# Regrouping the last rows of the output projection's weights: loads of 2, 1 and 1 rows, and rows 26 and 27 as one load

One Trainium2 chip, one core. The metric is the device time of the whole kernel in microseconds (us); a kernel's figure is the median of its runs. PE is TensorE (PEld its weight loads), DVE is VectorE, ACT ScalarE, POOL GpSimd, SP SyncE; SPq and ACTq stand for DMAs issued from SP and ACT. A load has landed when its semaphore has got the arrival of the last of the sixteen DMA engines.

## The reference, cut

```python
B, Sq, D = 32, 4, 1024;  Hq, Hkv, Sk, Dh = 32, 4, 2048, 128      # all bf16
q = (x @ wq).reshape(B, Sq, Hq, Dh).transpose(0, 2, 1, 3)
k, v = repeat(k_cache, 8, axis=1), repeat(v_cache, 8, axis=1)
p = softmax(einsum("bhqd,bhkd->bhqk", q, k) * Dh ** -0.5)
o = einsum("bhqk,bhkd->bhqd", p, v)
return o.transpose(0, 2, 1, 3).reshape(B, Sq, Hq * Dh) @ wo      # wo: 4096 x 1024
```

151 MB must be read, nearly all of it the two caches. `wo`, 8 MB, comes last.

## The kernel before

Everything is loaded by one queue, issued from SP in a fixed order: x, wq, the K and V caches batch by batch, then `wo`. In SBUF `wo` is 32 "rows" of 1024 columns on each of 128 partitions; one row is one step of the contraction of the output projection.

```python
WO = (4, 4, 4, 4, 4, 4, 2, 1, 1)          # rows 0 to 27, whole rows, so many to a load
NA = 768                                  # rows 28 to 31 come as columns 0:768, then 768:1024
LATE = 4
NB = NA + 144
COLS = ((0, 0, NA // 2), (512, NA // 2, NA), (1024, NA, NB), (1536, NB, D))
# ... (cut)
pieces = [(sum(WO[:c]), m, 0, D) for c, m in enumerate(WO)] \
       + [(u, 1, 0, NA) for u in range(Hq - LATE, Hq)] \
       + [(Hq - LATE, LATE - 1, NA, D), (Hq - 1, 1, NA, D)]       # (first row, rows, columns)
for c, (u, m, n0, n1) in enumerate(pieces):
    # ... (cut)   one load for each piece, with a semaphore of its own
# ... (cut)   the products: PE waits for the piece that holds row u's columns
for u in range(Hq - LATE):
    oproj(u, (0, 1, 2, 3))
for js in ((0, 1), (2, 3)):               # all of 0:768 first, then 768:1024
    for u in range(Hq - LATE, Hq):
        oproj(u, js)
# ... (cut)   oproj_out: PSUM to SBUF, then two stores
for j, eng in enumerate(("dve", "act", "act", "dve")):
    copy(eng, *COLS[j], j)
for j, (n0, n1, waits) in enumerate(((0, NA, (0, 1)), (NA, D, (2, 3)))):
    p.dma(("sp", "act")[j], ... out_flat[:, n0:n1] <- y_sb[:, n0:n1] ..., [("oe", i) for i in waits], ...)
```

So the tail has two halves: the first store (768 columns, from SP) can go while the last 256 columns are still being loaded and multiplied; the second store (256 columns, from ACT) ends the kernel.

## Time and profile before

| | before |
|---|---|
| median of the first three runs | 362.21 us (362.02 to 362.26) |
| span of the profiled run (first to last instruction), granted clock | 360.8 us, 1.0 |
| bytes read, mean rate over the span | 151.26 MB, 420 GB/s |
| last `wo` piece landed (all sixteen engines' parts) | 358.20 us |
| first, second store issued | 358.65, 359.08 us |

The page and the tail's timeline stand in the prediction below.

### The profile page before, as it was taken

The numbers are of one execution on the slowest core, as the hardware profiler recorded it, in microseconds if no ns is written. First come the engines' busy times: TensorE is split into PE (matmuls) and PEld (weight loads), VectorE is DVE, ScalarE is ACT, GpSimd is POOL, SyncE is SP. The second block draws the span as 40 slices with busy tenths as digits, with TensorE's granted clock in tenths as the row PEclk, the third lists the DMA queues.
The fourth block names the chain that finished last, engine by engine and source line by source line (L and its number), as shares of the span: only waits on it lengthen the run. The fifth ranks groups of instructions, "written<-read, shape, count | busy, mean of one in ns | idle before, by whom it ended". The sixth has DMA issues, their size and how long they took to land. (4 is left out here: it accounts for less than half of the span.)

```text
span 360.8 us, 6288 instructions
## 1 busy us (share of the span) xinstructions
PE 307.0 (85%) x3066; PEld 147.2 (41%) x2342; DVE 269.2 (75%) x171; ACT 103.0 (29%) x111; POOL 165.3 (46%) x262
## 2 busy tenths in 40 slices
PE   1988788999999999988999888888888898889896
PEld 1002000445444554444444444443333444448721
DVE  0018799999899888879999888888888888865600
ACT  1014222333333333333333333323222233333100
POOL 8002055255555555554455444455555554444100
PEclk9999999999999999999999999999999999999999
DMA  8999999999999999999999999999999999999996
GB/s 323 434 434 430 425 427 430 430 419 425 431 425 427 429 429 429 426 429 430 429 425 430 430 425 429 429 432 421 432 427 434 420 432 429 434 420 430 414 417 242
DMA packets 12651, 151.66 MB, mean 420 GB/s; under 512 B 1376, under 2 KB 2656, under 8 KB 3168
## 3 DMA queue, kind: packets, MB, share of 16 engines
q1 hardware_dynamic: 12496, 151.46, 99.1%
q8 instruction: 6, 0.10, 0.1%
q10 hardware_dynamic: 144, 0.07, 0.1%
q14 instruction: 5, 0.04, 0.0%
HBM read 151.26 MB, written 0.26 MB: 420 GB/s over the span
## 5 line engine op out<-in xcount | busy, mean ns | idle before, releaser
L329 DVE STREAM_TRANSPOSE KT_sb<-big 128x2048 f32<-128x2048 f32 x64 | 146.6, 2293 | 16.5 <-DMA big<-in_k_cache_dram 16.5
L355 ACT ACTIVATE P_sb<-ps_s,negmx 128x2048 bf16<-128x2048 f32 x32 | 82.1, 2566 | 184.7 <-DVE negmx L351 184.7
L16 PE MATMUL ps_s<-KT_sb,QD_sb 128*128 128x512 bf16 x384 | 103.7, 377 | 0.0
L386 POOL COPY PD_sb<-PT_sb 32x1024 f32<-32x1024 f32 x62 | 64.1, 1034 | 63.4 <-PE ps_r L395 60.5
L386 POOL COPY big<-PT_sb 32x1024 f32<-32x1024 f32 x61 | 63.1, 1034 | 58.9 <-PE ps_r L395 56.1
L351 DVE TENSOR_REDUCE negmx<-ps_s 128x1 f32<-128x2048 f32 x32 | 73.2, 2287 | 12.4 <-PE ps_s L16 10.7
L395 PE MATMUL ps_r<-big 128*128 128x128 bf16 x1024 | 59.8, 219 | 11.4 <-PEq L85 11.4
L395 PE MATMUL ps_r<-big,PD_sb 128*128 128x128 bf16 x1024 | 59.8, 219 | 9.9 <-PEq L85 9.9
L395 PEld LDWEIGHTS ps_r<-big 128*128 128x128 bf16 x1024 | 57.9, 98 | 22.1 <-issue 21.7
L395 PEld LDWEIGHTS ps_r<-big,PD_sb 128*128 128x128 bf16 x1024 | 58.0, 98 | 21.2 <-issue 20.7
L342 PE MATMUL ps_s<-KT_sb,QD_sb 128*128 128x512 bf16 x128 | 48.3, 377 | 18.1 <-PEq L85 18.1
L342 PEld LDWEIGHTS ps_s<-KT_sb,QD_sb 128*128 128x128 bf16 x128 | 12.3, 96 | 102.8 <-issue 102.8
L364 DVE STREAM_TRANSPOSE PT_sb<-P_sb 128x1024 f32<-128x1024 f32 x32 | 39.8, 1245 | 15.8 <-ACT P_sb L355 15.8
L319 POOL COPY QD_sb<-QT_sb 32x64 f32<-32x64 f32 x128 | 29.4, 229 | 46.1 <-DVE QT_sb L298 20.4
L16 PE MATMUL ps_r<-ident 128*128 128x384 bf16 x173 | 33.3, 325 | 0.0
L367 PEld LDWEIGHTS ps_r<-ssum,permf 128*128 128x128 f32 x64 | 11.9, 187 | 24.8 <-issue 23.1
L404 ACT ACTIVATE QT_sb<-ps_r,rinv 128x128 bf16<-128x128 f32 x32 | 11.7, 367 | 29.6 <-PE ps_r L395 27.3
L280 DVE TENSOR_SCALAR KT_sb<-ps_r 128x512 bf16<-128x512 f32 x2 | 1.3, 686 | 20.1 <-PE ps_r L264 20.1
L16 PE MATMUL ps_s<-big,KT_sb 128*128 128x384 bf16 (+2 forms) x92 | 14.1, 256 | 0.0
L421 PE MATMUL ps_s<-big,KT_sb 128*128 128x384 bf16 (+1 forms) x36 | 11.1, 317 | 2.1 <-DMA big<-in_wo_dram 1.1
L435 DVE CAST P_sb<-ps_s 128x384 bf16<-128x384 f32 (+1 forms) x2 | 0.8, 415 | 15.7 <-PE ps_s L421 15.4
L253 PE MATMUL ps_r<-ident 128*128 128x384 bf16 x32 | 10.3, 323 | 0.0
(41 smaller groups left out, 85.2 us busy)
## 6 DMA issues: line engine op xcount, KB each, us to landing
big<-in_k_cache_dram SPq DMA_DIRECT2D x32, 2048.0 KB, 18.5
big<-in_v_cache_dram SPq DMA_DIRECT2D x32, 2048.0 KB, 22.0
big<-in_wq_dram SPq DMA_DIRECT2D x4, 2048.0 KB, 14.0
big<-in_wo_dram SPq DMA_DIRECT2D x6, 1024.0 KB, 22.9
big<-in_wo_dram SPq DMA_DIRECT2D x5, 192.0 KB, 17.2
big<-in_wo_dram SPq DMA_DIRECT2D x1, 512.0 KB, 23.9
big<-in_wo_dram SPq DMA_DIRECT2D x2, 256.0 KB, 23.8
P_sb<-in_x_dram SPq DMA_DIRECT2D x1, 256.0 KB, 2.7
```

The costliest lines, as they stand in the source:

```text
L16: return eng.add_instruction(mybir.InstMatmult(name=nc.get_next_instruction_name(), engine=eng.engine, start_tensor_calc=start, stop_tenso ...
L319: p.op("pool", lambda e, s=src, d=dst: e.tensor_copy(d, s), waits if g == 0 else [("pt", i - 2)] * (g == 1 and i > 1), ("qd", i) if g == G ...
L329: p.op("dve", lambda e, s=src, d=dst: e.transpose(d, s), waits, ("kt", i, c), gives="t_kt" if c else None)
L342: mm = lambda e, a_=(out_, lhsT, rhs), f=first, l=last: e.matmul(a_[0], lhsT=a_[1], rhs=a_[2], start=f, stop=l, skip_group_check=True)
L351: p.op("dve", lambda e: e.tensor_reduce(negmx[:, i % 4:i % 4 + 1], ps_s[:, :], AX.X, ALU.max, negate=True), [("qk", i)], ("negmx", i))
L355: p.op("act", lambda e: e.activation(P_sb[:, :, :, :].rearrange("p t r w -> p t w r"), ps_s[:, :].rearrange("p (t w r) -> p t w r", w=2, r=R),
L364: p.op("dve", lambda e: e.transpose(dst, src), [("exp", i)], ("pt", i))
L367: p.op("pe", lambda e: e.matmul(ring[(i if i == L else i // 2 * 2) % 4][:, 510 + i % 2:511 + i % 2], lhsT=permf[:, :], rhs=ssum[:, i % 4:i ...
L386: p.op("dve" if i >= B - 2 and g < i - B + 4 else "pool", lambda e, s=src, d=dst: e.tensor_copy(d, s), [free] * (g == 0 or i >= B - 2) + [ ...
L395: p.op("pe", lambda e: e.matmul(buf[:, 0:Dh], lhsT=pd_of(i)[:, t // 2, :, :, :, t % 2].rearrange("p x g q -> p (x g q)"), rhs=big[:, slot_ ...
L404: p.op("act", lambda e: e.activation(dst, src, ACT.Copy, scale=rinv[:, i % 4:i % 4 + 1]), [("pv", i), ("rinv", i)], ("o", i))
L421: mm = lambda e, a=(out_, lhsT, rhs): e.matmul(a[0], lhsT=a[1], rhs=a[2], start=(u == 0), stop=(u == Hq - 1), skip_group_check=True)
```

## The change

The intent: let the last 256 columns of rows 28 and 29 land before row 30's, so that PE has less to do after the last byte; and save small packets with rows 26 and 27 in one load.

```diff
-    WO = (4, 4, 4, 4, 4, 4, 2, 1, 1)
+    WO = (4, 4, 4, 4, 4, 4, 2, 2)
@@
-        pieces = [...] + [(u, 1, 0, NA) for u in range(Hq - LATE, Hq)] + [(Hq - LATE, LATE - 1, NA, D), (Hq - 1, 1, NA, D)]
+        pieces = [...] + [(Hq - u, m, n0, n1) for n0, n1 in ((0, NA), (NA, D)) for u, m in ((4, 2), (2, 1), (1, 1))]
```

([...], the whole rows made from `WO`, is cut.) Three parts, then: rows 26-27 merged; the 768-column pieces 1, 1, 1, 1 become 2, 1, 1; the 256-column pieces 3, 1 become 2, 1, 1.

More of the change, by code (lines that the diff above doesn't have):

```diff
@@ L219, in bass_standalone__gqa_block_cached__sampling_kernel @@
         wo_v = wo.rearrange("(h p e) n -> p h (e n)", p=128, e=4)
-        pieces = [(sum(WO[:c]), m, 0, D) for c, m in enumerate(WO)] + [(u, 1, 0, NA) for u in range(Hq - LATE, Hq)] + [(Hq - LATE, LATE - 1, NA, D), (Hq - 1, 1, NA, D)]
+        pieces = [(sum(WO[:c]), m, 0, D) for c, m in enumerate(WO)] + [(Hq - u, m, n0, n1) for n0, n1 in ((0, NA), (NA, D)) for u, m in ((4, 2), (2, 1), (1, 1))]
         assert sum(WO) == Hq - LATE
```

## The prediction

> **What bounds the kernel now.** I read the page from the top: shares, slices, the DMA queues, then the chain that ended last, then the last microseconds in the timeline.
>
> ```profile
> span 360.8 us, 6288 instructions
> ...
> DMA  8999999999999999999999999999999999999996
> ...
> HBM read 151.26 MB, written 0.26 MB: 420 GB/s over the span
> ...
> DMA 8%; PE 3%; SPq 1%; issue 0%; DVE 0%
> DMA big<-in_wo_dram 8%; PE ps_r L395 1%; PE ps_s L16 1%; PE ps_s L421 1%; SPq L228 1%; SPq L212 0%; DVE P_sb L435 0%
> ```
>
> The DMA slice digits are 9 in all but the first and the last of 40 slices: the 16 DMA engines have work for the whole span, and 151 MB at 420 GB/s is the span. The change leaves the bytes alone, so it can win only in the tail. The chain in order of time says where the tail begins:
>
> ```profile
> 324.90 27.90 DMA big<-in_wo_dram
> 352.79 0.05 issue
> 352.84 0.34 PE ps_s L421
> ...
> 358.03 0.03 issue
> 358.06 0.24 PE ps_s L421
> ...
> 358.72 0.27 DVE P_sb L435
> ```
>
> It names the load that brings rows 20 to 23 (landed 352.79) and then gives 352.84 to 358.69 to PE. That is half the truth. Starts and waits in the timeline show that PE meets the loads again and again:
>
> ```profile
> 356.30 0.34 PEld L421 LDWEIGHTS ps_s<-big,KT_sb 128*128 128x128 bf16 x2 [0.34 <-DMA big<-in_wo_dram]
> ...
> 357.04 0.34 PE L421 MATMUL ps_s<-big,KT_sb 128*128 128x384 bf16 x1
> ...
> 357.53 0.10 PEld L421 LDWEIGHTS ps_s<-big,KT_sb 128*128 128x128 bf16 x1 [0.40 <-DMA big<-in_wo_dram]
> ...
> 358.06 0.24 PE L421 MATMUL ps_s<-big,KT_sb 128*128 128x144 bf16 x1
> ...
> 358.40 0.23 PE L421 MATMUL ps_s<-big,KT_sb 128*128 128x144 bf16 x1
> ...
> 358.65 0.35 SPq L440 DMA_DIRECT2D out_dram<-P_sb  x1
> 358.72 0.27 DVE L435 CAST P_sb<-ps_s 128x112 bf16<-128x112 f32 x1 [0.26 <-PE ps_s L16]
> 359.08 0.37 ACTq L440 DMA_DIRECT2D out_dram<-P_sb  x1
> ```
>
> The trace's semaphore events give each load's landing (its sixteenth arrival), in us: rows 24-25 at 354.09, 26 at 354.77, 27 at 355.45; the 768-column pieces of 28, 29, 30, 31 at 355.98, 356.50, 356.99, 357.48; the 256-column piece of rows 28-30 at 358.01, that of row 31 at 358.20. Matmuls start at 357.04, 357.53 and 358.06, each 0.05 us after the landings 356.99, 357.48 and 358.01. So at the very end the loads lead and PE follows. In the last step it is different: row 31's 256 columns landed at 358.20, but its matmul starts at 358.40, because PE was still doing rows 28 to 30, which it got only at 358.01. That 0.20 us is what the change goes for.
>
> **What the Trainium skill says.** (1) "DMA: Bandwidth & Descriptors", section "Why a DMA increments its semaphore by 16 and not by 1": the engines of one DMA finish independently, each adds one, and only the full 16 means that all has landed. The trace agrees: the arrivals of row 31's last piece spread from 356.54 to 358.20, so the slowest engine sets each landing and the fastest is done 1.66 us earlier. (2) Same page, "Why small descriptors are slow (HBM only)": each packet has a fixed overhead. The trace's packets took (median) 313 ns at 8192 B, 161 at 4096, 86 at 2048, 67 at 1536, 27 at 512: a slope of 152 ns for 4096 B and some 8 to 10 ns on top of each. (3) "Perfetto Trace Analysis", "DMA Optimizations": going from 2 KB to 4 KB "can dramatically improve throughput". Here it doesn't look so: two of 2048 B take 172 ns, one of 4096 takes 161, 6% less. (4) First page again, "Queues, rings and completion order": an engine takes turns between the queues it has work for. This matters for the two stores below; the trace of before can't show it well, as the second store's first packet starts at 360.02, when most of the first's are done.
>
> **The change part by part**, on the slowest engine, which serves 8 partitions, so 8 packets a row of wo.
>
> Rows 26 and 27 in one load. 16 packets of 2048 B become 8 of 4096 B, and one semaphore write (9 ns) goes. From landings: two one-row loads took 354.77 - 354.09 = 0.68 and 355.45 - 354.77 = 0.68, together 1.36; a load of the same form as the new one, rows 24-25, took 354.09 - 352.79 = 1.30. Gain 0.06: rows 26-27 land at 355.39. Row 26 now lands 0.62 later than before, but PE, 0.44 us a row, reaches it only at 355.47; no wait.
>
> The 768-column pieces as 2, 1, 1. Packets the same, 32 an engine; one semaphore write less (0.01). Four pieces took 0.53, 0.52, 0.49, 0.49. So rows 28-29 land at 355.39 + 1.04 = 356.43, row 30 at 356.92, row 31 at 357.41.
>
> The 256-column pieces as 2, 1, 1 in place of 3, 1. Packets the same (32 of 512 B), one semaphore write more. The three-row piece took 358.01 - 357.48 = 0.53, so 0.18 a row; rows 28-29 land at 357.77, row 30 at 357.95, row 31 at 358.14.
>
> PE, at 0.33 us for a 768-column row and 0.11 for a 256-column one, each start at least 0.05 after landing. Row 28 (768): 356.48, 0.13 later than the 356.35 of before, as it now waits for row 29 too. Row 29: 356.81; row 30: 357.13, data long there; row 31: max(357.46 from PE, 357.46 from its landing). Before: 357.53. The delay is made good by then, with nothing to spare. 256 columns: row 28 at 357.82, 29 at 357.93, 30 at 358.05, 31 at max(358.16, 358.14 + 0.05) = 358.19, where it was 358.40. So **PE ends 0.21 us earlier**; its last product of the 768 columns comes 0.07 earlier.
>
> What of 0.21 gets through. The first store (768 columns) hangs on row 31's 768 columns: issue 358.65 becomes 358.58. ACT copies the second half of these columns (358.07 to 358.56) and then the 144 columns at 358.67; moved 0.07, ACT is free at 358.49 and takes the 144 at about 358.50 where PE alone would allow 358.46. So the second store's issue moves by some 0.15 to 0.17, from 359.08 to 358.92. Then the stores meet: in the trace the first's packets run from 359.52 to 360.20 and the second's from 360.02 to 360.40. An engine needs 8 x 66 + 8 x 28 ns = 0.75 us for both, and 359.52 + 0.75 = 360.27 is close to the 360.40 of before, so the engines were nearly busy throughout. The end then moves by something between the 0.07 of the first store and the 0.16 of the second's issue: I take 0.12. Nothing else lies between: the block's closing semaphores are over at 359.86, and the last landing (360.77) ends the span.
>
> Sum: 362.21 - 0.12 = 362.09, call it **362.1 us**, 0.03% faster.
>
> **The rivals.** (a) PE takes over the wait: with the two-row piece, row 28 starts 0.13 late and the catching up fails, if landings come a bit later than worked out (a two-row piece interleaves rows and may be slower). Row 31's 768 columns would then stay at 357.53 or slip to 357.6, and the first store with it; time 362.2 to 362.3. For it: there is no slack in the sum. Against: landings of one-row pieces before show no gap between them. (b) The transfer is hidden anyway: the two stores run one after the other on the same engines, and only the first's 0.07 counts; 362.15. The packet times above speak for it in part, and it is in my 0.12. (c) SP hands out the loads too late. Its issues block (one of 6.29 us), so the queue is full, but the last issue ends at 351.69 and its packets run only after 355: over 3 us of margin, and 88 packets an engine for rows 24-31 become 80. Nothing to lose, nothing to win: 362.1. (d) All gains add up, 0.06 from the packets and 0.2 from PE, with no meeting of the stores: 362.0.
>
> **Range and chances.** The three runs of before lie 0.24 us apart, twice my expected gain, so the run-to-run spread sets the range: 361.75 to 362.4. A change of 2% would be 7.2 us; all that follows the touched loads' first landing is 8 us, of which the matmuls and stores stay. Faster by over 2%: 0.01; within 2%: 0.98; slower: 0.01.
>
> **What would show it right or wrong.** In the changed trace: eight packets of 4096 B an engine in place of sixteen of 2048, and a landing of rows 26-27 near 355.4 relative to rows 20-23 at 352.79; row 28's matmul waiting for a DMA near 356.48; the first 144-column matmul near 357.82 and the last near 358.19, some 0.37 apart where it was 0.35; the last 0.05 after a landing, not behind PE; the stores' issues less far apart (0.34 against 0.43) and their landings nearly together. A first 256-column start that isn't earlier than 358.0 would say that piece landings depend on the 16 engines' lag and not on the rows in the piece. A time outside 361.75 to 362.4 would mean that something before 352 us moved, which I exclude as no instruction there differs.

## More of the kernel before

One more view is of use, stretches of 1 us near the end: busy time of PE, PEld, DVE, ACT and POOL (with the number of instructions), then the granted clock, the mean busy share of the 16 DMA engines, and GB/s.

```profile
355.00:356.00 1.00, 1.00 (x12) 0.28 (x3) 0.00 (x0) 0.00 (x0) 0.00 (x0) 1.00 1.08 358
356.00:357.00 1.00, 1.00 (x10) 0.19 (x2) 0.00 (x0) 0.00 (x0) 0.00 (x0) 1.00 0.73 237
357.00:358.00 1.00, 1.00 (x5) 0.20 (x2) 0.09 (x1) 0.00 (x0) 0.00 (x0) 1.00 0.32 95
```

A share over 1 means that recorded packets overlap in time. The rate does not stop at once: from 356 us on the share falls to 0.73 and 0.32, because some engines are through with their part of the loads and others are not. The slowest engine decides each landing.

## The result, and the profile after

| | before | changed |
|---|---|---|
| median, six runs each | 362.19 us (362.02 to 362.30) | 362.12 us (361.99 to 362.23) |
| ratio | | 0.9998, 95% interval 0.9985 to 1.0011 |
| span of the profiled run | 360.8 us | 360.9 us |

A ratio here is the mean time of one kernel's fast runs over the mean of the other's of the same rounds, so not quite the ratio of the medians quoted. All runs were, those below too, at a granted clock of 1.0 or 0.999. The 0.07 us between the medians is below what the runs resolve, and the changed kernel's profiled run even has the longer span. What the change does has to be read from the tail.

The chain that ended last, of the changed kernel, in order of time (start, us, what):

```profile
325.12 27.86 DMA big<-in_wo_dram
352.99 0.05 issue
353.04 0.34 PE ps_s L421
...
358.72 0.02 issue
358.74 0.27 DVE P_sb L435
```

The chain has the same form, but rows 20 to 23 landed at 352.99 us where it was 352.79, though the change touches nothing that lands before. That shift of 0.20 us is larger than the effect we look for. So from here on **every time in the tail is counted from that landing and written with a plus sign**.

The timeline of the changed kernel:

```profile
356.65 0.34 PE L421 MATMUL ps_s<-big,KT_sb 128*128 128x384 bf16 x1
...
357.65 0.34 PE L421 MATMUL ps_s<-big,KT_sb 128*128 128x384 bf16 x1
...
358.02 0.24 PE L421 MATMUL ps_s<-big,KT_sb 128*128 128x144 bf16 x1
...
358.42 0.24 PE L421 MATMUL ps_s<-big,KT_sb 128*128 128x144 bf16 x1
...
358.77 0.35 SPq L440 DMA_DIRECT2D out_dram<-P_sb  x1
359.10 0.37 ACTq L440 DMA_DIRECT2D out_dram<-P_sb  x1
```

Row 28's matmul waits until 356.65 (+3.66), row 31's 768 columns start at 357.65 (+4.67; before 357.53, +4.74), the 256 columns run from 358.02 (+5.03; before +5.27) to a last start at 358.42 (+5.43; before +5.61). PE's last matmul starts 0.18 and ends 0.17 us earlier. The first store is issued at +5.79 (before +5.86), the second at +6.11 (before +6.29). But the end is at +7.94, before +8.02: 0.08 us. Where the rest of the 0.17 went is the question for the experiments.

### The profile page after: what moved, and what is told of

It is laid out like the page before. It is cut to its first block, busy times and chain, and to the rows that moved or that the text cites. A ratio compares the mean times of both kernels' runs of the same rounds, so it can differ in the third digit from the quotient of the medians.

```text
span 360.9 us, 6285 instructions
## 1 busy us (share of the span) xinstructions
PE 306.6 (85%) x3064; PEld 147.2 (41%) x2342; DVE 269.2 (75%) x171; ACT 102.9 (29%) x111; POOL 165.3 (46%) x262
```

## The experiments

Twelve runs were made, of ten altered kernels and of the two kernels once more, each with five rounds against the kernel before (na832 had six runs) and one profile, all correct. The device times lie so close that the table gives the tail of each profile. "P1" and "P2" are the first packets of the first and the second store, taken from the trace's DMA records; landings are the trace's semaphore events; "end" is the end of the span. Only the two kernels themselves have two profiles; every other row rests on one.

| run | rows 20-23 landed, us | row 31 (768) starts | last 256-col. start | 1st store issued | 2nd store issued | P1 | P2 | end |
|---|---|---|---|---|---|---|---|---|
| before | 352.79 | +4.74 | +5.61 | +5.86 | +6.29 | +6.71 | +7.23 | +8.02 |
| before_again | 352.85 | +4.73 | +5.60 | +5.85 | +6.27 | +6.70 | +7.22 | +8.01 |
| changed | 352.99 | +4.67 | +5.43 | +5.79 | +6.11 | +6.63 | +7.15 | +7.94 |
| after_again | 353.16 | +4.65 | +5.38 | +5.77 | +6.06 | +6.62 | +7.14 | +7.93 |
| merge_only | 353.05 | +4.65 | +5.54 | +5.77 | +6.21 | +6.62 | +7.14 | +7.92 |
| split768_only | 352.77 | +4.77 | +5.64 | +5.89 | +6.32 | +6.74 | +7.26 | +8.04 |
| split256_only | 352.86 | +4.73 | +5.50 | +5.85 | +6.19 | +6.70 | +7.22 | +8.01 |
| last256_one | 352.85 | +4.75 | +5.81 | +5.86 | +6.48 | +6.72 | +7.37 | +8.14 |
| big_pieces | 352.91 | +5.71 | +6.37 | +6.82 | +7.05 | +7.67 | +8.19 | +8.97 |
| rows256_each | 352.91 | +4.66 | +5.43 | +5.78 | +6.11 | +6.63 | +7.15 | +7.94 |
| na704 | 352.70 | +4.45 | +5.30 | +5.50 | +6.04 | +6.35 | +6.95 | +7.74 |
| na832 | 352.77 | +4.73 | +5.34 | +5.90 | +5.98 | +6.75 | +7.28 | +8.04 |
| before_onestore | 352.74 | +4.76 | +5.63 | none | +6.26 | none | +7.14 | +8.36 |
| after_onestore | 352.74 | +4.67 | +5.41 | none | +6.06 | none | +6.93 | +8.14 |

### Both kernels once more: before_again and after_again

No edit. For before_again:

> Before unaltered: a second profile of it and five more rounds against itself. Counted from the landing of rows 20 to 23. Theory (the tail repeats itself, the landing scatters): last matmul start +5.61, stores +5.86 and +6.29, end +8.02, each within 0.03 us; the landing anywhere from 352.7 to 353.2. Rival (single profiles scatter in the tail too): end anywhere from +7.9 to +8.1, and the difference of 0.09 to the changed kernel means nothing.

For after_again:

> The changed kernel unaltered, to see what one profile and five rounds are worth. Theory: counted from the landing of rows 20 to 23 the tail repeats that of the first profile (last matmul start +5.43, stores +5.79 and +6.11, end +7.94) within 0.03 us, while the landing itself may lie elsewhere by 0.2 us; time 0.0 to 0.2 us under before. Rival: the tail's own figures scatter by 0.1 us, and no step of the prediction can be read from single profiles.

Measured: 362.16 us (362.05 to 362.60; the rounds' own before 362.17) and 362.22 us (362.00 to 362.40; before 362.16). The ends repeat to 0.02 us, +8.02 and +8.01 against +7.94 and +7.93, and the stores' issues to 0.02 or, for the second, 0.05; the last matmul of the changed kernel scattered as much, +5.43 and +5.38, more than the 0.03 expected. The landing of rows 20 to 23 scattered by 0.17 us between the changed kernel's two profiles. So the tail's 0.08 us is real, and the whole time can't show it: with five more rounds the changed kernel's median was 362.22.

### merge_only: only rows 26 and 27

```diff
-    WO = (4, 4, 4, 4, 4, 4, 2, 1, 1)
+    WO = (4, 4, 4, 4, 4, 4, 2, 2)
```

> Only rows 26 and 27 become one load. Times below are counted from the landing of rows 20 to 23, which in the profile of before is at 352.79 us; before: last matmul starts at +5.61, first store issued at +5.86, second at +6.29, end at +8.03. Theory (steps of the prediction): everything after the merged load moves by the 0.06 us of the packets: last matmul +5.55, end +7.97. Rival 1 (the packets give the whole gain): end +7.94, as in the changed kernel. Rival 2 (packets give nothing at the landing): end +8.03. Time within 0.1 us of before in every case; the trace decides.

Measured: 362.20 us (before in these rounds 362.14), end +7.92. Rows 26-27 landed at +2.57 where row 27 alone had landed at +2.65; row 31's 768 columns started 0.09 earlier, the first store went 0.09 earlier, and the end came 0.10 earlier. That is rival 1: this part alone gives what the whole change gives, although PE's last matmul starts only 0.08 earlier than before (the changed kernel: 0.18). Its timeline (its rows 20-23 landed at 353.05):

```profile
358.58 0.23 PE L421 MATMUL ps_s<-big,KT_sb 128*128 128x144 bf16 x1
...
358.82 0.35 SPq L440 DMA_DIRECT2D out_dram<-P_sb  x1
...
359.26 0.37 ACTq L440 DMA_DIRECT2D out_dram<-P_sb  x1
```

### split768_only

```diff
-  [(u, 1, 0, NA) for u in range(Hq - LATE, Hq)]
+  [(Hq - u, m, 0, NA) for u, m in ((4, 2), (2, 1), (1, 1))]
```

> Only the 768-column pieces become 2, 1, 1 rows. Same reference point. Theory: row 28's matmul waits some 0.15 to 0.2 us longer for a DMA (start +3.75 where it was +3.55), PE has made it good by row 31 (start +4.74, as before), last matmul +5.60, end +8.02. Rival (the delay is not made good and the first store slips): row 31 at +4.9, end +8.2 or later.

Measured: 362.18 us (before 362.14), end +8.04. Row 28 waited until +3.73 (before +3.55); by row 31 all but 0.03 us of that was made good (+4.77), and those 0.03 delayed the first store. The end came 0.02 or 0.03 later, by the first or the second profile of before. This part costs a little or nothing.

### split256_only

```diff
-  [(Hq - LATE, LATE - 1, NA, D), (Hq - 1, 1, NA, D)]
+  [(Hq - u, m, NA, D) for u, m in ((4, 2), (2, 1), (1, 1))]
```

> Only the 256-column pieces become 2, 1, 1 rows. Theory: first of the 256-column matmuls at +5.10 instead of +5.27, last at +5.47 instead of +5.61, waiting for its landing and not for PE; second store +6.18, first store unchanged at +5.86; the stores share the engines, so the end gains only a part: +7.96. Rival 1 (stores do not meet): end +7.90. Rival 2 (piece size does not set landings): first matmul stays at +5.27, end +8.03.

Measured: 362.18 us (before 362.14), end +8.01. Its timeline (its rows 20-23 landed at 352.86):

```profile
357.97 0.24 PE L421 MATMUL ps_s<-big,KT_sb 128*128 128x144 bf16 x1
...
358.37 0.24 PE L421 MATMUL ps_s<-big,KT_sb 128*128 128x144 bf16 x1
...
358.72 0.35 SPq L440 DMA_DIRECT2D out_dram<-P_sb  x1
359.05 0.37 ACTq L440 DMA_DIRECT2D out_dram<-P_sb  x1
```

On PE it does just what was meant: first start +5.11 where it was +5.27, last +5.50 where it was +5.61, second store issued 0.10 earlier. Then the gain vanishes: P2 is at +7.22, before +7.23. My theory gave the end half of it (+7.96); it got 0.01. This part is worth nothing at the end, and not because piece sizes do not matter (rival 2) but because of what comes after the issue.

The table says what. In ten of the twelve profiles with two stores, P2 comes 0.52 or 0.53 us after P1, whenever the second store was issued: 0.43 us after the first (before), 0.33 (changed) or 0.08 (na832). On each engine the first store is eight packets of 1536 B at 66 ns, 0.53 us (na832: 1664 B at 69 ns, 0.55). The trace's DMA queues, for the changed kernel in 359.60 to 360.12 us, that is from P1 until just before P2 (queue: packets, MB, share of the 16 engines; q1 is SP's queue, q10 ACT's):

```profile
q1 hardware_dynamic: 116, 0.18, 94.9%
```

And in 360.12 to 360.60:

```profile
q10 hardware_dynamic: 144, 0.07, 49.2%
q1 hardware_dynamic: 28, 0.02, 12.7%
```

The second store had been issued at 359.10, and a single store's first packet came 0.87 us after its issue (after_onestore), which would be 359.97. Until 360.12 not one of its packets moves. When the first of them starts, at 360.14, 118 of the first store's 128 packets have started and three of its sixteen engines have come to the semaphore write that closes their share (in all ten profiles: 118 to 121 packets, one to three engines). So it looks as if an engine takes the second store's packets when it is through with its share of the first. The packet records carry no engine number, so this is not seen engine by engine; and whether the second store waits at the engines or just before them, its transfers being made ready late, no run here separates. So the second theory: **the end is P2 + 0.76 to 0.79, and P2 is the later of P1 + 0.52 and the second issue + 0.87 to 0.91** (0.91 is na704's, below). Before the change the first of the two holds, and PE's work on the 256 columns has slack.

### last256_one: the opposite dose

```diff
-  [(Hq - LATE, LATE - 1, NA, D), (Hq - 1, 1, NA, D)]
+  [(Hq - LATE, LATE, NA, D)]
```

> The opposite dose: the 256 columns of all four rows as one load, all else as before. Theory: the first of their matmuls waits for the last byte: start +5.45, last start +5.79 (0.17 later than before); the second store moves out of the first's shadow, so the end takes the full delay: +8.18, time 0.15 us over before. Rival (the last landing alone sets the end, whatever the pieces): last start +5.61, end +8.02.

Measured: 362.29 us (before 362.14; the interval of the ratio holds 1), end +8.14, short of the +8.18 expected.

```profile
358.31 0.24 PE L421 MATMUL ps_s<-big,KT_sb 128*128 128x144 bf16 x1 [0.21 <-DMA big<-in_wo_dram]
...
358.66 0.23 PE L421 MATMUL ps_s<-big,KT_sb 128*128 128x144 bf16 x1
358.71 0.36 SPq L440 DMA_DIRECT2D out_dram<-P_sb  x1
...
359.33 0.37 ACTq L440 DMA_DIRECT2D out_dram<-P_sb  x1
```

PE stands still for 0.21 us for the one load, the last matmul starts 0.20 later, the second store is issued 0.20 later, at 359.33. Of that, 0.14 arrives at P2 and 0.11 at the end: P2 is +7.37, 0.89 after the issue and 0.65 after P1. Now the second issue is the later of the two. The slack of the kernel before was thus about 0.06 us by P2 and 0.08 by the end, which is why a gain there is worth nothing and a loss is.

### big_pieces: a dose above the noise

```diff
-  [(u, 1, 0, NA) for u in range(Hq - LATE, Hq)] + [(Hq - LATE, LATE - 1, NA, D), (Hq - 1, 1, NA, D)]
+  [(Hq - LATE, LATE, 0, NA), (Hq - LATE, LATE, NA, D)]
```

> A dose above the noise: the 768 columns of rows 28 to 31 as one load, their 256 columns as another. Counted from the landing of rows 20 to 23 (before: +5.61 last matmul start, +5.86 and +6.29 the stores, +8.03 the end). Theory (PE follows the landings, and each piece costs PE the work on its rows after the landing): row 28's 768 columns start at +4.7, row 31's at +5.7, last 256-column matmul at +6.3 to +6.4, first store +6.8, end +8.8 to +8.9; time 0.75 to 0.9 us over before. Rival (transfers or stores hide it): time within 0.2 us of before.

Measured: 363.19 us (363.15 to 363.22) against 362.16 (362.05 to 362.27); ratio 1.0029, interval 1.0015 to 1.0042. The only run whose interval excludes 1.

```profile
357.63 0.34 PE L421 MATMUL ps_s<-big,KT_sb 128*128 128x384 bf16 x1 [1.01 <-DMA big<-in_wo_dram]
...
359.73 0.35 SPq L440 DMA_DIRECT2D out_dram<-P_sb  x1
359.95 0.37 ACTq L440 DMA_DIRECT2D out_dram<-P_sb  x1
```

PE follows the landings, so the rival falls. The end moved by 0.95 us: that is the first store's delay (0.96), not that of the second (0.76) nor of the last matmul (0.76). The estimate of 0.75 to 0.9 was low for that reason; the medians differ by 1.03.

### before_onestore and after_onestore

```diff
-  for j, (n0, n1, waits) in enumerate(((0, NA, (0, 1)), (NA, D, (2, 3)))):
-      p.dma(("sp", "act")[j], ...
+  for j, (n0, n1, waits) in enumerate(((0, D, (0, 1, 2, 3)),)):
+      p.dma("act", ...
```

(and the last wait is for one store.) For before_onestore:

> Before, with a single store of all 1024 columns after the last copy, in place of two stores. Theory: store issued at +6.29, end 0.2 to 0.35 us later than before, +8.25 to +8.38. Its partner is the next run.

For after_onestore:

> The changed kernel with a single store. Theory (half of PE's gain is lost where the two stores share the engines): with one store there is nothing to share, so the end lies 0.15 to 0.18 us nearer to the landing of rows 20 to 23 than in the run before this one, where with two stores the difference was 0.09. Rival (the gain is lost elsewhere, in the copies or in the landing of the last packets): the difference is 0.05 to 0.10 here too.

Measured: 362.46 us (362.39 to 362.63) and 362.27 us (362.17 to 363.12, the last a single run outside); ends +8.36 (within the +8.25 to +8.38 expected) and +8.14. The stores' lines, of before_onestore and then of after_onestore:

```profile
359.00 0.37 ACTq L440 DMA_DIRECT2D out_dram<-P_sb  x1
```

```profile
358.80 0.37 ACTq L440 DMA_DIRECT2D out_dram<-P_sb  x1
```

With nothing to queue behind, PE's gain reaches the end whole: the store is issued and the tail ends 0.21 us earlier (a little more than the 0.15 to 0.18 expected). The medians differ by 0.19, which the runs do not resolve. With two stores the same edit gave 0.08. The gain is lost where the second store waits behind the first, not in the copies or in the landings.

### rows256_each: still finer

```diff
-  ... for n0, n1 in ((0, NA), (NA, D)) for u, m in ((4, 2), (2, 1), (1, 1))]
+  ... 768 columns as in the changed kernel ... + [(u, 1, NA, D) for u in range(Hq - LATE, Hq)]
```

> The changed kernel with one load for each row of the 256 columns (1, 1, 1, 1 in place of 2, 1, 1). Theory: PE is at work on the 768 columns until +5.01 and the last row's landing sets the last matmul, so nothing is to be had: first 256-column start +5.01 to +5.03, last +5.40 to +5.44, end +7.93 to +7.96. Rival (finer pieces go on paying): last start +5.3, end +7.85.

Measured: 362.15 us, first 256-column start +5.00, last +5.43, end +7.94. As the theory had it, nothing more is to be had from this finer step. The last matmul's start shows it; the end alone would not, as it hangs on the first store.

### na704 and na832: another cut between the stores

```diff
-    NA = 768
-    NB = NA + 144
+    NA = 704              # na832: 832
+    NB = NA + 176         # na832: NA + 104
```

For na704:

> The changed kernel with the columns cut at 704 instead of 768, so that the first store is smaller and leaves earlier. Theory (the first store's packets hold up the second's: first packet of the second 1.04 us after its issue where one without a rival needed 0.87): first store issued near +5.60, second near +6.15, its first packet near +7.03, end +7.87 to +7.92. Rival (no hold-up; the second store's own time sets the end): the second issue is 0.04 later, so the end is too, +7.97.

For na832:

> The opposite: the columns cut at 832. Theory: first store issued near +5.97, second near +6.2, its first packet held up until some +7.35, end near +8.05, 0.1 later than the changed kernel. Rival (no hold-up): second store small and early, end +7.9.

Measured: na704 361.97 us (361.74 to 362.03), na832 362.20 us (362.05 to 363.73), before in these rounds 362.17 (362.02 to 362.52); ratios 0.9994 (0.9981 to 1.0007) and 1.0009 (0.9995 to 1.0022; one run of 363.73 pulls it up). The run of na704 that was profiled was its fastest. Of na704 (its rows 20-23 landed at 352.70):

```profile
357.99 0.25 PE L421 MATMUL ps_s<-big,KT_sb 128*128 128x176 bf16 x1
...
358.20 0.35 SPq L440 DMA_DIRECT2D out_dram<-P_sb  x1
...
358.74 0.37 ACTq L440 DMA_DIRECT2D out_dram<-P_sb  x1
```

The stores are now 0.54 us apart instead of 0.33. P2 follows its own issue by 0.91, the hold-up is gone, and the end is +7.74: 0.20 before the changed kernel, 0.29 before the old one, and better than the +7.87 to +7.92 expected. Of the 0.20, 0.13 is the hold-up (P2 1.04 us after the issue in the changed kernel, 0.91 here); 0.07 is the earlier issue, which goes back to a last landing at +5.25 where the kernels with the changed pieces and the cut at 768 had +5.33 to +5.38. I can't explain that landing and have one profile of it. na832 makes the opposite case: its second store was issued 0.13 earlier than the changed kernel's, at +5.98 (+6.2 was expected), had to wait 1.30 us for its first packet, and the end was 0.10 later, much as the first store was issued 0.11 later. Both rivals, which have no hold-up, fall. na704 is the best version by its trace and by its median; the interval of its ratio still holds 1.

## Why the prediction was right or wrong

**The size: right.** 362.1 was forecast and 362.12 measured, with "within 2%" at 0.98. The time itself could hardly have missed, as the effect is smaller than the runs' spread, and a hit to 0.02 us is luck: five more rounds of the same kernel gave 362.22. The steps are the better test.

**What bounds the kernel, and "PE follows the loads" at the end: right.** big_pieces and last256_one move PE by the landings.

**The merged load, 0.06: right, slightly small.** In the seven profiles that have it the merged rows landed at +2.55 to +2.60; in the seven that don't, row 27 landed at +2.64 to +2.65. About 0.07.

**The timetable of PE: right to 0.03 us.** Counted from the forecast's own reference, 352.79, it had row 28 at +3.69, row 31 at +4.67, the first and the last 256-column start at +5.03 and +5.40. Measured +3.66, +4.67, +5.03, +5.43; row 31's last columns landed at +5.38, so the last matmul now follows its landing, as forecast, and starts 0.18 earlier where 0.21 was forecast. Rival (a), a failed catching up, fell; in split768_only, where no merged load helps, 0.03 us of it is to be seen.

**"What of 0.21 gets through": the step that failed.** The prediction let the end move by "something between the 0.07 of the first store and the 0.16 of the second's issue" and took 0.12. Measured: 0.08. Its rival (b), "only the first's 0.07 counts", is what happens. The argument was that an engine is "nearly busy throughout" and that the two stores mix; in fact the second store moves nothing until 0.52 us after the first store's first packet, when the first engines are through with their share of it, so the second's earlier issue counts nothing while it comes early enough. (The first store's first packet starts at 359.50, not at 359.52 as the prediction has it; nothing hangs on that.) Hence the gain comes from the merged load alone, through row 31's 768 columns and the first store; the 2, 1, 1 of the 256 columns, the heart of the change, gives nothing (split256_only: 0.01), and the 2, 1, 1 of the 768 columns costs 0.02 to 0.03.

**"Their landings nearly together": wrong,** for the same reason. The stores' issues came 0.33 us apart as forecast (0.34), but they landed at 360.68 and 360.88, 0.20 apart, as before (0.22).

**The spread sets the range: right, and what scatters is now visible.** Over the 14 profiles the sixteenth arrival of rows 20-23 lies between 352.70 and 353.16 us, but the mean of the sixteen arrivals only between 351.86 and 352.04. What scatters is how far the slowest engine lags behind the mean (0.79 to 1.12 us). In the kernel before, the sixteen arrivals of a load are 0.48 us apart until the load that landed at 52.59, and 1.44 in the next, at 58.52. In between, 54 to 59 us, one packet of instructions is moved:

```profile
q1 hardware_dynamic: 143, 2.08, 98.4%
q8 instruction: 1, 0.02, 1.3%
```

Its record has 16384 B in 1.02 us. In split256_only there is none in that stretch; there the first one comes at 64.5 us, in 62 to 68:

```profile
q1 hardware_dynamic: 174, 2.59, 101.7%
q8 instruction: 1, 0.02, 1.1%
```

And there the arrivals stay 0.35 us apart up to the load that landed at 62.27, and are 1.45 apart in the next, at 68.34. It is so in all fourteen profiles: eleven have their first q8 packet at 55.9 to 56.6 us and the jump in the load that lands at 58.5 to 58.9, three (split256_only, rows256_each, na832) have it at 64.5 to 64.6 and the jump at 68.3 to 68.5. The Trainium skill, "Runtime: NRT & Kernel Launch", section "Instruction fetch mechanics", says that instructions are refilled in blocks of 16 KiB over DMA, and the size of the q8 packets agrees; those of a second instruction queue, q14, have 8192 B. That these fetches make the lag is an inference from times that coincide in every trace; no run took a fetch away, so it stays open. Why the lag near the end differs from run to run stays open as well.

Open too: the time gain of the changed kernel, which no number of rounds used here separates from zero.

## What to carry to other kernels

Before cutting the last pieces of a load finer, follow the gain to the end of the kernel: an earlier last matmul is worth nothing if its store then queues behind another store on the same engines. With two closing stores, look when the first packets of each move and not when they are issued, and cut the work so that the second is issued about one store's transfer time after the first (na704). For effects below the run-to-run spread, count times from the last event that the change cannot touch, and profile each kernel twice.

## What the Trainium skill lacked or had wrong

- "DMA: Bandwidth & Descriptors", section "Queues, rings and completion order": engines take turns between queues by whole packets of many descriptors, a part that the prediction left out. I read it as a mixing of two small stores; here the second store's first transfer came 0.52 to 0.53 us after the first store's, about as long as the eight transfers of an engine's share take (66 ns each at 1536 B), even when it was issued only 0.08 us later. This agrees with the page if all eight are one packet in its sense (what the profile calls a packet would be a descriptor there), but no page spells out that a short second store waits for the whole share of the first.
- "Runtime: NRT & Kernel Launch", section "Instruction fetch mechanics", calls the cost of a 16 KiB refill "mostly hidden". In this kernel, where the DMA engines are busy throughout, a refill's packet took 1.02 us where a load's packet of the same 16384 B takes 0.61, and the spread of the next load's sixteen arrivals went from 0.48 to 1.44 us (coincidence in time, in all fourteen profiles; not tested by itself).
- "Perfetto Trace Analysis", section "DMA Optimizations": from 2 KB to 4 KB "can dramatically improve throughput". Read as the size of a packet, here two of 2048 B took 172 ns and one of 4096 B took 161, and merging two such loads was worth 0.07 us.
- No page gives the size of it: how unevenly the 16 engines of one core run. A load's sixteen arrivals were 1.8 to 2.2 us apart near the end, and the slowest was 0.79 to 1.12 us behind their mean.
